# Gate and value of the first batch on 16-bit weight parts that later batches reuse, and the scores of two row blocks in one run

## The chip, the cores and the metric

One core of a Trainium2 chip runs the whole program. The metric is the time of one execution on the device in microseconds (us), as the median of the runs shown; one execution was recorded by the hardware profiler.

## What is computed

Four batches (B = 4) go through three blocks: causal attention over 8 heads of 64 with a second read from a memory matrix, a block of two linear maps whose product goes through w3 and w_out, and a gated block (gate, val, out).

```python
def _attn_ref(q, k, v, M_prev, z_prev, beta) -> np.ndarray:
    scores = scale * np.matmul(q, k.transpose(0, 1, 3, 2))
    ...
    a /= a.sum(-1, keepdims=True) + 1e-09
    local = np.matmul(a, v)
    ...
    return (g * mem_out + (1 - g) * local).astype(np.float32)

def _moe_ref(x, w1, w2, w3, w_out) -> np.ndarray:
    a = x @ w1
    b = x @ w2
    h = a * b @ w3
    return (h @ w_out).astype(np.float32)

def _moe2_ref(x, w_gate, w_val, w_out) -> np.ndarray:
    gate = 1.0 / (1.0 + np.exp(-(x @ w_gate)))
    val = x @ w_val
    return (gate * val @ w_out).astype(np.float32)
```

Each batch has 576 tokens of 512 features; w1 and w2 are 512 by 1024, gate and val 512 by 1536. The weights arrive as 64-bit numbers that the kernel itself converts to float32.

## The kernel before

**Products.** Every large product is split into parts: a weight is a large part plus a rest (`hi`, `lo`), an activation too, and `prod` issues three matmuls of 128x128 weights by 288 tokens (hi by hi, lo by hi, hi by lo). Parts are either float32 numbers rounded for the matmul unit (fp32r, `split_rows`: ScalarE casts, VectorE subtracts) or 16-bit floats after a multiplication by a power of two (`split_scaled`: ScalarE scales to the hi part, VectorE makes the rest). `power` works a scale out of a sum over partitions: `total` lets TensorE multiply a matrix of ones by one column, and four small VectorE instructions, each of which reads what the one before wrote, make the scale and its inverse.

**Stages.** `ffn(b)` runs four stages for batch b, and the trace shows each as one stretch of TensorE's time: `ab` (x by w1 and w2), `xw` (h by the product of w3 and w_out), `gv` (gate and val) and `ot` (the output map). In batch 0 the stretches are `ab` 118 to 219 us, `xw` 219 to 257, `gv` 257 to 334 and `ot` 334 to 386. The attention of batch b + 1 is fed into the stages of batch b piece by piece (`drive`), so its matmuls stand between those of the products; in the `gv` stages none does.

**Weights of batch 0.** A *unit* is 8 blocks of 128x128, for instance the gate and val blocks of one of the 12 column groups f. After every sixth matmul `pump` makes one step of each of three queues: `conv_step` converts half a unit from 64 bits (two ScalarE instructions, one VectorE instruction, and for `gv` units a VectorE maximum into `mcol`), `split_step` splits half a unit into fp32r parts in a ring of 5 slots (`wslot`), and `late_step` works on later batches' weights. In batch 0 one `gv` unit is two slots and one pass of f is 48 matmuls. Converted units are also stored whole (`kept`).

**Late tasks.** After batch 0's `gv` stage `late_scales` works out the scales of all 20 units of `ab` and `gv` at once. Then `late_split` reads the stored units back, 12 of them for `gv` first, makes 16-bit parts ("P", later sums "S") and stores these; batch 1 and later read them (`load_step`).

**PSUM.** Products and `total` take their banks from one pool, `ps_f`, of three buffers; which of them a tile gets is fixed when the program is built. A bank is free when ScalarE or VectorE has read what is in it. TensorE's order is the order written in the code. The other engines' orders are fixed when the program is built, and an engine that waits at one instruction starts none behind it.

**Scores.** `s_part(p, i, n)` makes the scores of row block i (116 rows, i + 1 column blocks) of the head pair p: three terms of two matmuls, one for each head, into two banks, then one VectorE instruction for each head, which adds the mask and takes the extreme value.

Of the kernel before, what the change touches and what calls it, by code (L numbers as in the profile page):

```python
# [19 lines left out]
T = 116  # L20
# [12 lines left out]
PB = 5  # L33
# [30 lines left out]
def tile_attention_memory_ffn(  # L64
# [178 lines left out]
    tasks = [(u, "P") for u in jobs[:F2]] + [(("o", *x), "P") for x in pairs_of]  # L243
# [135 lines left out]
    def conv_step():  # L379
# [27 lines left out]
        elif ws["step"] == 1:  # L407
# [50 lines left out]
    def split_step():  # L458
# [5 lines left out]
        u, hf = divmod(s, 2)  # L464
        r = raws[u][:, 4 * hf : 4 * hf + 4, :]
# [291 lines left out]
    def ffn(b):  # L757
# [3 lines left out]
        if b == 1:  # L761
            o2_scale()
            ws["limit"], ws["pace"] = NFIRST, PACE[5]
        if b == 2:
            ws["pace"] = PACE[3]
        if b > 0:
            htop = fp.tile([128, F1], F32, tag="htop", name=f"htop{b}", bufs=1)
        for f in range(F1):
# [36 lines left out]
            if b > 0:  # L805
                largest(htop[:, f : f + 1], hraw, AX.X)
# [12 lines left out]
        for d in range(KC):  # L819
            if b > 0 and d == 1:  # L820
                x2back = finish_x2(b, x2s)
                if b == 1:
# [698 lines left out]
```

## Time and profile before

| | us |
|---|---|
| three runs | 1014.47, 1018.92, 1017.41 (median 1017.41) |
| the profiled execution | 1013.13 |
| span from its first to its last instruction | 1011.3 |
| TensorE busy within the span | 982.4 (97%) |
| VectorE busy | 731.3 (72%) |
| ScalarE busy | 596.6 (59%) |
| GpSimd busy | 195.0 (19%) |

Busy time counts what an engine executes; a matmul is pipelined and the profile draws its end from a model, so that consecutive matmuls overlap and their spacing is read from start to start. Instructions of VectorE and ScalarE overlap too where they stand back to back.

### The profile page before, as it was taken

Reading aid. Unit: us, or ns where it says so; the run is one execution under the profiler, and the core shown is the slowest. Engines: PE = TensorE matmul, PEld = TensorE weight load, DVE = VectorE, ACT = ScalarE, POOL = GpSimd, SP = SyncE. Lnnn points to the kernel's source line nnn. Section 1 sums busy time; section 2 is a strip of 40 time slices with the busy share of each in tenths; the row PEclk is TensorE's granted clock in tenths of the full one; section 3 lists DMA queues with packets and bytes.
Section 4 is the critical chain, followed back from the end, with each engine's and each line's share of the span. In section 5 each row is a group of like instructions: output and inputs, shape, how many; then the busy total and the mean of one; then the engine's idle time right before and its main releaser. Section 6 shows DMA issues by size and latency. Waiting matters only on the chain. (4 is left out here: it accounts for less than half of the span.)

```text
span 1011.3 us, 19894 instructions
## 1 busy us (share of the span) xinstructions
PE 982.4 (97%) x7351; PEld 797.9 (79%) x7351; DVE 731.3 (72%) x1702; ACT 596.6 (59%) x1213; POOL 195.0 (19%) x196
## 2 busy tenths in 40 slices
PE   7999999999999999999999999999999999999998
PEld 3556687888999898898977777778777667797776
DVE  6866788777778826777777668988876757737883
ACT  7987787567777735564654545555655545324451
POOL 3454012213000101312200011343111311201110
PEclk9989999999999999999999999999999999999999
DMA  8865799967777249877887576655655556556532
GB/s 293 245 230 192 247 346 310 326 206 254 249 250 247 98 137 380 286 226 238 297 310 261 176 251 240 214 190 184 200 181 178 185 157 204 186 174 246 183 131 79
DMA packets 95642, 227.21 MB, mean 225 GB/s; under 512 B 11192, under 2 KB 39992, under 8 KB 95288
## 3 DMA queue, kind: packets, MB, share of 16 engines
q1 hardware_dynamic: 95544, 225.93, 66.3%
q8 instruction: 58, 0.95, 0.4%
q14 instruction: 40, 0.33, 0.1%
HBM read 164.55 MB, written 61.34 MB: 223 GB/s over the span
## 5 line engine op out<-in xcount | busy, mean ns | idle before, releaser
L532 PEld LDWEIGHTS <-wslot 128*128 128x128 f16 x1680 | 162.9, 98 | 49.7 <-issue 8.3
L1200 POOL TENSOR_SCALAR p<-p,sm,omg 116x116 f32<-116x116 f32 (+4 forms) x100 | 89.0, 895 | 406.2 <-DVE sm L1198 294.9
L521 PE MATMUL gv<-x,wslot 128*128 128x288 f32 (+1 forms) x1152 | 147.5, 290 | 0.2 <-ACT gsb L137 0.2
L521 PEld LDWEIGHTS <-wslot 128*128 128x128 f16 x1152 | 111.1, 98 | 32.1 <-issue 4.5
L532 PE MATMUL gvp<-x,wslot 128*128 128x288 f16 x1008 | 125.2, 286 | 3.6 <-ACT x L180 1.6
L137 ACT ACTIVATE p<-p,sm 116x116 f32<-116x116 f32 (+4 forms) x160 | 93.2, 585 | 46.6 <-DVE sm L1174 46.5
L521 PE MATMUL ot<-hg,wslot 128*128 128x288 f16 (+1 forms) x864 | 118.1, 291 | 0.0
L521 PE MATMUL ab<-x,wslot 128*128 128x288 f32 x768 | 117.2, 302 | 0.5 <-ACT asb L800 0.3
L521 PE MATMUL xw<-h,wslot 128*128 128x288 f32 x768 | 113.0, 300 | 1.7 <-ACT h L721 1.0
L521 PEld LDWEIGHTS ab<-x,wslot 128*128 128x128 f32 x768 | 104.0, 188 | 6.3 <-issue 2.9
L521 PEld LDWEIGHTS xw<-h,wslot 128*128 128x128 f32 x768 | 103.4, 188 | 5.5 <-issue 2.0
L1174 DVE CUSTOM_DVE_ANT_0 p<-s,msk 116x116 f32<-116x116 f32 (+4 forms) x160 | 68.0, 452 | 30.8 <-PE s L1169 26.8
L532 PE MATMUL abp<-x,wslot 128*128 128x288 f16 x672 | 87.1, 286 | 1.3 <-DVE u2ab L603 1.1
L723 DVE TENSOR_TENSOR wslot<-wraw,wslot 128x512 fp32r<-128x512 f32 x76 | 54.9, 725 | 34.7 <-ACT wslot L721 34.4
L521 PEld LDWEIGHTS gv<-x,wslot 128*128 128x128 f32 x576 | 76.4, 188 | 0.5 <-ACT gsb L137 0.5
L1230 PE MATMUL t<-idf,p 116*116 116x116 f32 x480 | 68.7, 272 | 3.3 <-DVE p L1200 2.5
L1230 PEld LDWEIGHTS t<-idf,p 116*116 116x116 f32 x480 | 54.3, 139 | 18.0 <-issue 5.3
L402 ACT ACTIVATE cy<-r 128x512 f32<-128x512 f32 x76 | 51.5, 678 | 13.3 <-DVE wraw L411 2.6
L721 ACT CAST wslot<-wraw 128x512 fp32r<-128x512 f32 x76 | 47.1, 621 | 16.2 <-PE gv L521 7.4
L411 DVE SCALAR_TENSOR_TENSOR wraw<-cy,cr 128x512 int32<-128x512 int32 x76 | 54.2, 740 | 2.6 <-ACT cr L403 2.1
L521 PE MATMUL wps<-wo,wslot 128*128 128x512 f32 x192 | 52.2, 407 | 0.0
L1248 ACT COPY pt<-t 116x696 f32<-116x696 f32 (+2 forms) x74 | 47.5, 650 | 7.4 <-PE t L1230 7.1
(210 smaller groups left out, 1630.0 us busy)
## 6 DMA issues: line engine op xcount, KB each, us to landing
wslot<-k SPq DMA_DIRECT2D x40, 512.0 KB, 4.3
wslot<-ka SPq DMA_DIRECT2D x40, 512.0 KB, 4.4
wrawl<-kf SPq DMA_DIRECT2D x32, 512.0 KB, 6.1
wslot<-kb SPq DMA_DIRECT2D x40, 384.0 KB, 3.5
k<-wslot SPq DMA_DIRECT2D x24, 512.0 KB, 4.7
r<-in_gv_dram SPq DMA_DIRECT2D x24, 512.0 KB, 5.1
kf<-wraw SPq DMA_DIRECT2D x20, 512.0 KB, 3.5
ka<-wS SPq DMA_DIRECT2D x20, 512.0 KB, 4.4
```

The source lines that it names most:

```text
L137: ins = nc.scalar.activation(**kw)
L402: nc.scalar.activation(out=y, in_=hi, func=AF.Prelu, scale=2.0**-112, alpha=2.0**32)
L411: nc.vector.scalar_tensor_tensor(z, y, 3, tmp["r"], ALU.logical_shift_left, ALU.bitwise_or)
L521: paced["pe"] = nc.tensor.matmul(ps, w[:, wi, blk, :], x[:, xi, cols : cols + n], start=first and part == 0, stop=last and part == 2,)
L532: paced["pe"] = nc.tensor.matmul(ps, w[:, wi, blk + k, :], x[:, xi, k, :], start=not more and k == 0 and part == 0, stop=k == 1 and part == 2,
L721: nc.scalar.copy(dst[:, 0], src)
L723: eng.tensor_sub(dst[:, 1], src, dst[:, 0].bitcast(F32))
L1174: nc.vector.tensor_tensor_reduce(out=ps_[hh][:, c0:c1], in0=os_[hh], in1=msk[:, SP - w + c0 : SP - w + c1], scale=-0.125, scalar=3.0e38 if ...
L1200: lower(SHARE_N).tensor_scalar(ps_[hh][:, :w], ps_[hh][:, :w], sm[:, 6 + hh : 7 + hh], omg[:T, 2 * p + hh : 2 * p + hh + 1], ALU.mult, ALU ...
L1230: nc.tensor.transpose(tp[:T, c : c + T], src[hh][:, j * T : (j + 1) * T], idf[:T, :T])
L1248: nc.scalar.copy(to, got)
```

## The change

In batch 0 the `gv` units are no longer split into fp32r halves. `scaled_step` works out a scale for each unit on its own (`unit_scale`: one `total` of two matmuls and the four small instructions), splits the whole unit in one go into 16-bit parts, which fill one slot of the ring, and stores them for the later batches. The 12 late tasks that made these parts are gone. Since 16-bit weights need 16-bit activations, the result of `xw` in batch 0 is scaled too, with a bound that needs the maximum of each h (`htop`) and the power of that bound. The scale of each unit enters the sigmoid and the product through `x2back`.

Apart from that, for batches 1 to 3 the scores of row blocks 0 and 1 are made in one run of twelve matmuls into the same two banks. The pool of score tiles grows from 5 to 6, and q's natural-order tile goes from two buffers to one.

```diff
-    tasks = [(u, "P") for u in jobs[:F2]] + [(("o", *x), "P") for x in pairs_of]
+    tasks = [(("o", *x), "P") for x in pairs_of]
...
+    def unit_scale(u):
+        n = rank[u]
+        power(wsc[:, n : n + 1], wsc[:, NJ + n : NJ + n + 1], total(f"wsum{n}", *(mcol[:, hf, n : n + 1] for hf in range(2))))
+        scaled.add(u)
+
+    def scaled_step(u, now):
+
+        if ws["conv"] < 2 * u + 2:
+            return False
+        if u not in scaled:
+            if not now and ws["pumps"] < ws["ready"]:
+                return False
+            unit_scale(u)
+            return True
+        if in_use("wslot") >= RING:
+            return False
+        w = fp.tile([128, 2, 8, 128], F16, tag="wslot", name=f"wslot{ws['ring']}", bufs=RING)
+        split_scaled(w[:, 0], w[:, 1], raws.pop(u), wsc[:, rank[u] : rank[u] + 1])
+        nc.sync.dma_start(out=whole16[u]["P"], in_=w)
+        done.append((u, "P"))
+        put("wslot", [w])
+        ws["split"] += 2
+        return True
...
+        if u in rank and rank[u] < F2:
+            return scaled_step(u, now)
...
-            if b > 0:
-                largest(htop[:, f : f + 1], hraw, AX.X)
+            largest(htop[:, f : f + 1], hraw, AX.X)
...
-                if b == 0:
-                    nc.scalar.copy(xt[:, 0, c0 : c0 + HS], ps[:, :HS])
-                    nc.vector.tensor_sub(
-                        xt[:, 1, c0 : c0 + HS], ps[:, :HS], xt[:, 0, c0 : c0 + HS].bitcast(F32)
-                    )
-                elif b == 1 and d == 0:
+                if b < 2 and d == 0:
                     nc.scalar.copy(x20[:, c0 : c0 + HS], ps[:, :HS])
-                elif b == 1:
+                elif b < 2:
                     split_scaled(xt[:, 0, c0 : c0 + HS], xt[:, 1, c0 : c0 + HS], ps[:, :HS], x2s[:, 0:1])
...
+            s = take(1)
+            if b == 0:
+                slot(s)
+                nc.vector.tensor_mul(x2back[:, f : f + 1], wsc[:, NJ + f : NJ + f + 1], x2s[:, 1:2])
...
+            if i == 1 and not first:
+                return
+            rows = (0, 1) if i == 0 and not first else (i,)
```

**VectorE in the `gv` stage.** Before, one pass of f looks like this on VectorE (`wslot` is the rest of half a unit, `hgraw` the gated product, `wraw` a conversion, `mcol` a maximum, `hg` the rest of the gated activations):

```order
L964 TENSOR_TENSOR hgraw0_5_3659<-gv0_5_0_1_3687,gsb0_5_0_3685 128x288
L723 TENSOR_TENSOR wslot55_3726<-wraw31_3495,wslot55_3726 128x512
L964 TENSOR_TENSOR hgraw0_5_3659<-gv0_5_1_1_3719,gsb0_5_1_3717 128x288
L411 SCALAR_TENSOR_TENSOR wraw34_3753<-cy68_3735,cr68_3736 128x512
L411 SCALAR_TENSOR_TENSOR wraw34_3753<-cy69_3765,cr69_3766 128x512
L723 TENSOR_TENSOR wslot56_3756<-wraw32_3581,wslot56_3756 128x512
L176 TENSOR_REDUCE mcol_86<-wraw34_3753 128x1
L723 TENSOR_TENSOR hg0_5_3658<-hgraw0_5_3659,hg0_5_3658 128x576
L176 TENSOR_REDUCE mcol_86<-wraw34_3753 128x1
```

With the change, early in the same stage, `pw`, `wsc` and `x2back0` being the small instructions of a scale (the first `wsc` row of each `pw` makes the scale, the second its inverse):

```order
L164 TENSOR_SCALAR wsc_83<-pw_3354 128x1
L165 TENSOR_SCALAR pw_3354<-wsc_83 128x1
L985 SCALAR_TENSOR_TENSOR hgraw0_0_3286<-gv0_0_1_1_3344,x2back0_2897,gsb0_0_1_3342 128x288
L166 TENSOR_SCALAR wsc_83<-pw_3354 128x1
L163 TENSOR_SCALAR pw_3391<-wsum4_3388 128x1
L969 TENSOR_TENSOR x2back0_2897<-wsc_83,x2s0_2813 128x1
L164 TENSOR_SCALAR wsc_83<-pw_3391 128x1
L181 SCALAR_TENSOR_TENSOR wslot43_3365<-wraw27_3111,wsc_83,wslot43_3365 128x1024
L165 TENSOR_SCALAR pw_3391<-wsc_83 128x1
L749 TENSOR_TENSOR hg0_0_3285<-hgraw0_0_3286,hg0_0_3285 128x576
L439 SCALAR_TENSOR_TENSOR wraw30_3402<-cy60_3382,cr60_3383 128x512
L166 TENSOR_SCALAR wsc_83<-pw_3391 128x1
```

The two halves became one instruction of twice the width, and the small instructions of two scales stand around it. The rest `wslot43` reads ScalarE's hi part of the same unit, and that hi part reads the scale of the first row shown; `wslot44`, whose scale is the `wsc` row just ahead of `wslot43`, follows two rows after the last one shown.

**ScalarE at the start of `gv`.** Before, `wslot` being the hi part of half a unit, `x2_0_3` the last block of `xw`, `cy` and `cr` a conversion and `gsb` a sigmoid, with the load of its table ahead of the first:

```order
L841 CAST x2_0_3_3155<-xw0_3_0_3156 128x288
L721 CAST wslot43_3205<-wraw25_2856 128x512
L721 CAST wslot44_3229<-wraw26_2992 128x512
L841 CAST x2_0_3_3155<-xw0_3_1_3192 128x288
L402 ACTIVATE cy58_3305<-r64_58_3167 128x512
L403 ACTIVATE cr58_3306<-r64_58_3167 128x512
L402 ACTIVATE cy59_3335<-r64_59_3218 128x512
L403 ACTIVATE cr59_3336<-r64_59_3218 128x512
L137 ACT_TABLE_LOAD
L137 ACTIVATE gsb0_0_0_3258<-gv0_0_0_0_3236 128x288
```

With the change:

```order
L180 ACTIVATE wslot41_3210<-wraw25_2864,wsc_83 128x1024
L180 ACTIVATE x2_0_3_3182<-xw0_3_0_3183,x2s0_2813 128x288
L180 ACTIVATE wslot42_3246<-wraw26_3028,wsc_83 128x1024
L430 ACTIVATE cy58_3277<-r64_58_3140 128x512
L431 ACTIVATE cr58_3278<-r64_58_3140 128x512
L180 ACTIVATE x2_0_3_3182<-xw0_3_1_3236,x2s0_2813 128x288
L430 ACTIVATE cy59_3304<-r64_59_3224 128x512
L431 ACTIVATE cr59_3305<-r64_59_3224 128x512
L137 ACT_TABLE_LOAD
L137 ACTIVATE gsb0_0_0_3310<-gv0_0_0_0_3288,x2back0_2897 128x288
```

Two hi parts of whole units, each behind the scale that VectorE makes, stand ahead of the table load, and one of them ahead of the last block's first half. In the program as built, `gv0_0_1_0` (the gate product of the second token half) has the bank of `gv0_0_0_0` with the change, and so waits for the first sigmoid; before it had a bank of its own, and the product behind it waited for that sigmoid.

**TensorE, scores of batch 2, pair 1.** Before, row block 0 is one run and row block 1 another, with products between them:

```order
L1169 MATMUL s2_1_0_0_0_5250<-qkh2_1_5194,qkl2_1_5195 116x116
L1169 MATMUL s2_1_0_0_1_5251<-qkh2_1_5194,qkl2_1_5195 116x116
L1169 MATMUL s2_1_0_0_0_5250<-qkl2_1_5195,qkh2_1_5194 116x116
L1169 MATMUL s2_1_0_0_1_5251<-qkl2_1_5195,qkh2_1_5194 116x116
...
L1169 MATMUL s2_1_1_0_0_5321<-qkh2_1_5194 116x232
L1169 MATMUL s2_1_1_0_1_5322<-qkh2_1_5194 116x232
L1169 MATMUL s2_1_1_0_0_5321<-qkh2_1_5194,qkl2_1_5195 116x232
L1169 MATMUL s2_1_1_0_1_5322<-qkh2_1_5194,qkl2_1_5195 116x232
```

With the change they stand in one:

```order
L1201 MATMUL s2_1_1_0_0_5348<-qkl2_1_5289,qkh2_1_5288 116x116
L1201 MATMUL s2_1_1_0_1_5349<-qkl2_1_5289,qkh2_1_5288 116x116
L1201 MATMUL s2_1_1_0_0_5348<-qkh2_1_5288 116x232
L1201 MATMUL s2_1_1_0_1_5349<-qkh2_1_5288 116x232
L1201 MATMUL s2_1_1_0_0_5348<-qkh2_1_5288,qkl2_1_5289 116x232
L1201 MATMUL s2_1_1_0_1_5349<-qkh2_1_5288,qkl2_1_5289 116x232
L1201 MATMUL s2_1_1_0_0_5348<-qkl2_1_5289,qkh2_1_5288 116x232
```

The first run's last pair is followed at once by the second block's first.

## Rows read from the trace of the kernel before

**Rows 1.** Windows: busy time, granted clock and DMA load in five stretches
```profile
core 0: us, PE busy (x) PEld busy (x) DVE busy (x) ACT busy (x) POOL busy (x), PEclk, DMA share, GB/s
219.00:257.00 38.00, 36.34 (x282) 32.29 (x281) 30.39 (x74) 26.79 (x58) 9.86 (x8) 1.00 0.75 260
257.00:334.00 77.00, 76.76 (x580) 76.53 (x578) 60.52 (x109) 58.15 (x110) 0.00 (x0) 1.00 0.72 245
334.00:386.00 52.00, 50.84 (x378) 46.84 (x378) 24.52 (x51) 25.24 (x45) 6.00 (x4) 0.97 0.41 139
386.00:466.00 80.00, 79.29 (x618) 69.42 (x618) 59.38 (x160) 48.17 (x106) 22.12 (x20) 1.00 0.81 282
...
347.60:351.00 3.40, 3.40 (x17) 3.07 (x18) 3.40 (x9) 1.25 (x2) 1.19 (x1) 0.51 0.40 154
```

**Rows 2.** Groups by line and shape: the `gv` matmuls on fp32r and 16-bit parts
```profile
L521 PE MATMUL gv<-x,wslot 128*128 128x288 f32 x576 | 76.7, 295 | 0.2 <-ACT gsb L137 0.2
L521 PE MATMUL gv<-x,wslot 128*128 128x288 f16 x576 | 70.8, 286 | 0.0
```

**Rows 3.** Timeline of VectorE over one pass of f in batch 0
```profile
283.42 0.45 DVE L964 TENSOR_TENSOR hgraw<-gv,gsb 128x288 f32<-128x288 f32 x1
283.79 1.28 DVE L411 SCALAR_TENSOR_TENSOR wraw<-cy,cr 128x512 int32<-128x512 int32 x2
284.99 0.68 DVE L723 TENSOR_TENSOR wslot<-wraw,wslot 128x512 fp32r<-128x512 f32 x1
285.59 0.68 DVE L176 TENSOR_REDUCE mcol<-wraw 128x1 bf16<-128x512 f32 x1
286.19 0.75 DVE L723 TENSOR_TENSOR hg<-hgraw,hg 128x576 fp32r<-128x576 f32 x1
...
287.45 0.45 DVE L964 TENSOR_TENSOR hgraw<-gv,gsb 128x288 f32<-128x288 f32 x1
289.17 0.69 DVE L723 TENSOR_TENSOR wslot<-wraw,wslot 128x512 fp32r<-128x512 f32 x1 [1.27 <-ACT wslot L721]
```

**Rows 4.** Timeline of VectorE and ScalarE where batch 1 makes its x2 scale
```profile
475.54 0.14 DVE L163 TENSOR_SCALAR pw<-x2sum 128x1 int32<-128x1 int32 x1
475.72 0.15 DVE L164 TENSOR_SCALAR x2s<-pw 128x1 f32<-128x1 f32 x1
...
475.99 0.78 ACT L180 ACTIVATE x<-x,x2s 128x576 f16<-128x576 f32 x1
```

**Rows 5.** Timeline of VectorE in batch 1's `gv` stage
```profile
521.11 0.51 DVE L960 SCALAR_TENSOR_TENSOR hgraw<-gv,x2back,gsb 128x288 f32<-128x288 f32 x1
521.53 0.14 DVE L1030 TENSOR_SCALAR hgs<-hgs 128x1 f32<-128x1 f32 x1
521.61 1.28 DVE L181 SCALAR_TENSOR_TENSOR wS<-wrawl,wsc,wS 128x1024 f16<-128x1024 f32 x1
522.81 0.81 DVE L181 SCALAR_TENSOR_TENSOR hg<-hgraw,hgs,hg 128x576 f16<-128x576 f32 x1
```

**Rows 6.** Groups by line and shape: ScalarE's part of a 16-bit split
```profile
L180 ACT ACTIVATE wP<-wrawl,wsc 128x1024 f16<-128x1024 f32 x12 | 13.8, 1148 | 4.9 <-DMA wrawl<-kf 4.9
```

**Rows 7.** Timeline of TensorE and ScalarE at the start of batch 0's `gv` stage
```profile
257.27 4.92 PE L521 MATMUL gv<-x,wslot 128*128 128x288 f32 x36
262.42 3.84 PE L521 MATMUL gv<-x,wslot 128*128 128x288 f32 x27 [0.24 <-ACT gsb L137]
...
260.67 1.28 ACT L137 ACT_TABLE_LOAD   x1
261.96 0.71 ACT L137 ACTIVATE gsb<-gv 128x288 f32<-128x288 f32 x2
```

**Rows 8.** Timeline of TensorE around a score block in batch 1's `ab` stage
```profile
418.84 2.24 PE L521 MATMUL ab<-x,wslot 128*128 128x288 f32 x15
421.00 0.37 PE L1169 MATMUL s<-qkh 64*116 64x232 f32 x2
```

**Rows 9.** Timeline of TensorE at a wait in batch 0's `ot` stage
```profile
347.06 0.90 PE L1169 MATMUL s<-qkh 64*116 64x290 f32 x2 [1.16 <-DVE sm L1174]
```

More of the change, by code (lines that the diff above doesn't have):

```diff
@@ L271, in tile_attention_memory_ffn @@
     wot = {}
-    ws = {"conv": 0, "step": 0, "split": 0, "ring": 0, "freed": 0, "use": 0, "again": 0, "pumps": 0, "late": 0, "task": 0, "part": 0, "limit": 0, "pace": 0, "tops": 0, "wo": 0, "pass": 0, "wready": False}
+    ws = {"conv": 0, "step": 0, "split": 0, "ring": 0, "freed": 0, "use": 0, "again": 0, "pumps": 0, "late": 0, "task": 0, "part": 0, "limit": 0, "pace": 0, "ready": 0, "tops": 0, "wo": 0, "pass": 0, "wready": False}
     tmp = {}
+    scaled = set()
     last = {}
@@ L327, in late_split @@
         late_o2 = u not in rank
+        if late_o2 and "o2" not in scaled:
+            scaled.add("o2")
+            o2_scale()
+            return
         by = o2s[:, 0:1] if late_o2 else wsc[:, rank[u] : rank[u] + 1]
@@ L456, in load_step, with split_step @@
         return True
-    def split_step():
+    def split_step(now=False):
         s = ws["split"]
@@ L1173, in s_part @@
[L1173 to L1183 removed]
+            if i == 1 and not first:
+                return
@@ new lines, in s_part @@
+            os_ = [
+                ps_s.tile([128, 512], F32, tag="s", name=f"s{b}_{p}_{i}_{n}_{hh}")[:T, :at] for hh in range(2)
+            ]
+            terms = [(qks[p], qks[p])] if first else [(parts[p][x], parts[p][y]) for x, y in ((0, 0), (1, 0), (0, 1))]
+            for i, w, c0, c1, at in jobs:
+                for x, (q_, k_) in enumerate(terms):
+                    for hh in range(2):
+                        r = slice(64 * hh, 64 * hh + 64)
+                        nc.tensor.matmul(
+                            os_[hh][:, at : at + c1 - c0], q_[r, 0, i * T : (i + 1) * T], k_[r, 1, c0:c1],
+                            start=x == 0, stop=x == len(terms) - 1,
+                        )
@@ new lines, in s_part @@
+            for i, w, c0, c1, at in jobs:
+                ps_, sm = sp[p, i]
+                for hh in range(2):
+                    nc.vector.tensor_tensor_reduce(
+                        out=ps_[hh][:, c0:c1],
+                        in0=os_[hh][:, at : at + c1 - c0],
+                        in1=msk[:, SP - w + c0 : SP - w + c1],
+                        scale=-0.125,
+                        scalar=3.0e38 if n == 0 else sm[:, 2 * hh : 2 * hh + 1],
+                        op0=ALU.add,
+                        op1=ALU.min,
+                        accum_out=sm[:, 2 * hh + n : 2 * hh + n + 1],
+                    )
```

110 lines of the change are left out of this document (45 added, 65 removed).

## The prediction, made before the changed kernel ran

> **What bounds the kernel now.** The table of the profile comes first: TensorE is busy in 97% of the span, so a change counts where it alters what TensorE executes or makes it wait. Next come the windows, one for each stage [rows 1]. In batch 0's `gv` stage (257 to 334 us) TensorE is busy for 76.76 of 77.00 us at full granted clock, VectorE for 60.52, ScalarE for 58.15, and DMA at a share of 0.72. So TensorE sets the pace there, one pass of f in 6.4 us, and VectorE, with 79%, is the engine with the least room. The groups by line [rows 2] hold what the change can gain: the same 576 matmuls take 76.7 us on fp32r parts in batch 0 and 70.8 us on 16-bit parts in batch 1, 133 against 123 ns each. With 16-bit parts TensorE wants a pass in 5.9 us.
>
> The timeline of VectorE [rows 3] shows what one pass costs there, read from start to start, since durations overlap by about 0.08 us: two conversions 1.20, two rests of half a unit 1.20, two maxima 1.20, two `hgraw` 0.74, one `hg` 0.67: 5.0 us of work in 6.4. The rest is waiting, for example 1.27 us for ScalarE's hi part of a `wslot`.
>
> **The change, part by part.** The sum is made against the profiled execution, 1013.13 us, which is 4.3 us below the median of the runs, 1017.41; the differences are then laid on the median.
>
> *Matmuls of `gv`.* -5.9 us on TensorE [rows 2], if it is fed. Nine of the twelve pairs that sum for the scales stand in this stage. No row has such a pair; two matmuls at 133 ns give 0.27 as an upper bound, and nothing is the lower one; I take 0.1 each, since they have one column instead of 288. So TensorE would need 71.7 us.
>
> *VectorE in `gv`.* From the first half of `hgraw0_0` to the rest `wslot51`, the last split, VectorE's list in the changed program holds 16 conversions and 18 maxima at 0.60 [rows 3], 16 `hgraw` that now multiply by `x2back` as well, at 0.42 (521.11 to 521.53 [rows 5]), 7 `hg` at 0.67, 9 rests of whole units at 1.20 (521.61 to 522.81 [rows 5]), and 46 small instructions. The first five kinds come to 9.6 + 10.8 + 6.7 + 4.7 + 10.8 = 42.6 us. The grouping itself gains nothing here: two halves cost 1.20 and so does a whole. A small instruction takes 0.08 us with independent work behind it (521.53 to 521.61 [rows 5]) and 0.18 where the next reads its result (475.54 to 475.72 [rows 4]): 3.7 to 8.3 us for 46. Some stand in a chain and others between large instructions, so I take 6.0.
>
> A rest also waits for ScalarE's hi part, and that for the scale: 0.27 us from the scale's instruction to ScalarE's start (475.72 to 475.99 [rows 4]) and 1.15 for the hi part [rows 6], 1.42 in all, less what VectorE does meanwhile. Behind the scale of `wslot43` stand one `hgraw` and five small instructions, about 1.07, so a wait of 0.35; `wslot45` is alike, and before `wslot51` there is about 0.8, a wait of 0.6. Before the other six stands a whole split, an `hg` or a conversion, more than 1.42. That is 1.3 us, if ScalarE comes to the hi part at once. Sum: 42.6 + 6.0 + 1.3 = 49.9 us.
>
> TensorE consumes eight units meanwhile, for which it would need 47.8. So **VectorE becomes the pace of these eight units**, barely. How much it idles besides is not to be read: nothing at best, and at worst the 1.3 to 1.4 us that each pass idles now, 10 us for eight. Most of that idling exists because TensorE is the pace now, so it should shrink; I take 3.8.
>
> *The start of `gv`.* ScalarE loads its table (1.28 us) ahead of the first sigmoid, which starts 4.69 us after the stage's first matmul; TensorE goes on 5.15 us after it [rows 7]. Today that costs 0.24 us, because 36 matmuls run before its result frees a bank. In the changed program the third product has the bank of the first, so 24 matmuls run, 2.95 us. At an unchanged time of the sigmoid that is a wait of 2.2 us. The two hi parts of whole units in front take 1.15 each instead of 0.62 for halves, so it could come 1.1 us later (3.3); or earlier, as the scales of these units are summed long before the stage begins and ScalarE can do both hi parts in `xw` (1.1). I take 2.2: VectorE's row above then starts 5.15 us into the stage.
>
> *The stage's end.* 5.15 + 49.9 + 3.8 = 58.9 us for the rest `wslot51`. The last read of unit 7's products stands 2.2 us ahead of it (three small instructions, the wait, the split), at 56.7. TensorE is by then perhaps one product (1.5 us) into unit 8 and has four units to do, 23.6 us, for which VectorE has no splits left: 56.7 - 1.5 + 23.6 = 78.8. That is **2.0 us longer than today's 76.8**: the gain of 5.9 is spent. Without idling it is 75.0, with all of it 85.2.
>
> *A rule on small instructions.* The Trainium skill, page "Perfetto Trace Analysis", section "Optimizing Scalar/DVE Operations", gives about 60 ns of overhead for each VectorE instruction on SBUF and says that grouping helps a saturated engine. By it the 46 would cost 2.8 us instead of 6.0, and the stage would come out at 75.6, which makes the whole 1014.5. The row of independent work (0.08) is near it and the row of a dependent chain (0.18) is not; these are chains.
>
> *`xw` of batch 0.* VectorE has one maximum more ahead of what `xw` begins with (0.60 [rows 3]), and the bound and its power follow; then three sums for scales stand in the stage. VectorE is at 80% in `xw` [rows 1]. I take +0.8 us, between 0 and 2.
>
> *`ab` of batch 0.* Eight maxima for `htop`, 4.8 us of VectorE, hidden by its idle time; in batch 1's `ab` VectorE is busy for 59.38 of 80 us [rows 1]. +0.3, at most 4.8 if that cover is gone.
>
> *The late tasks.* Twelve hi parts (13.8 us [rows 6]) and twelve rests (14.4) vanish. They lie in `ot` of batch 0 and `ab` of batch 1, where ScalarE and VectorE have room and TensorE is idle for 1.16 and 0.71 us only [rows 1]: 0, at best -1.9. The 12 loads go too, and the stores move into `gv`.
>
> *Scores in one run.* TensorE needs 2.16 us for 15 matmuls up to a score block [rows 8], 0.165 us more than 15 times 133 ns: the price of turning to another shape. A run spared saves that once, or twice if turning back costs as much: 12 head pairs (three batches) make 2.0 to 4.0 us; I take -2.8. VectorE's first mask instruction then comes six matmuls later; the next products of that bank pair are further away. q's single buffer could delay a load; nothing shows that, and I put it at 0.
>
> **Sum:** +2.0 + 0.8 + 0.3 - 2.8 = +0.3 us, 1013.4 for the profiled execution, **1018 us** on the median.
>
> **The rivals.** *VectorE keeps up (faster).* If it hardly idles and the first sigmoid comes early, `gv` takes 71.7 plus about 1.1: -4.0. With +1.1 for `ab` and `xw`, -2.8 for the scores and -1.9 for the late tasks this is -7.6, 1010 us. For it: eight units need 47.8 against 49.9 us, close. Against it: VectorE is at no more than 80% in any whole stage of [rows 1]. It decides if VectorE's work and waits of one unit stay below 5.9 us. Chance 0.16.
>
> *The way through ScalarE becomes the bound (slower).* The 1.42 us are hidden only if ScalarE takes up each hi part as soon as its scale is there. ScalarE's list has sigmoids, conversions and `hg` ahead of it. If it comes to each hi part late, VectorE stands still for 1.42 at each of the nine splits: 12.8 instead of 1.3. Replacing the 3.8 of idling too, `gv` takes 86.5, +9.7, and the whole +8.0, 1025 us. For it: VectorE waits 1.27 us for ScalarE's hi part already now, with half the width [rows 3]. Against it: ScalarE is busy for only 58.15 of 77 us [rows 1]. It decides if three or more of the splits show such a wait over 1 us. Chance 0.22. The Trainium skill ("Perfetto Trace Analysis", section "Per-instruction lifecycle: what the profiler-reported window actually captures") calls the queues of these two engines strict FIFO; that is this rival's rule, and the trace agrees so far as that 1.27 us wait holds up everything behind it.
>
> *The DMA becomes the bound (slower).* 245 GB/s at a share of 0.72 [rows 1] make about 340 at a full one. A unit now moves 1.05 MB in, 0.52 out as before, and 0.52 of 16-bit parts out: 2.1 MB, 6.2 us. Conversions run up to a unit further ahead than before; nine units of it take 55.8 us less 4.7 for what the three load buffers hold, 51, against VectorE's 49.9. At worst it adds 5 us: 1023. Chance 0.10.
>
> *Waits bring the clock down (slower).* After the 1.16 us wait at 347.06 [rows 9] the granted clock is 0.51 for 3.4 us [rows 1], the lower level of 1.2 GHz, which costs 1.7 us. Five waits of that length in `gv` would add 8.5: 1026. In today's `gv` the clock stays at 1.00. Chance 0.08.
>
> That the change doesn't do what it says is hardly possible: batch 1 runs the same matmuls at 16 bits already.
>
> **How the numbers follow.** The forecast (VectorE paces at about the old rate) has 0.44. 0.5%, or 5.1 us, is about what a measurement of this kernel can tell from no change. Faster by more: 0.16, the first rival. Slower by more: the ScalarE and the clock rival, half of the DMA rival, less a bit for their mild forms, 0.31. Within: 0.53. The likeliest case's own range is 1013 to 1023 (idling from 0 to 8 us in `gv`); for 8 in 10 it reaches to the first rival below and beyond the ScalarE rival above: **1010 to 1029**.
>
> **What would show it.** In the changed profile: 576 16-bit matmuls in batch 0's `gv`, with about 123 ns each where they run unhindered; a wait on a sigmoid of some 2 us in front of the third product; VectorE busy above 85% until `wslot51`, TensorE waiting for `hgraw` or sigmoids in these units and not in the last four; the stage some 79 us long; 12 fewer score runs. I am wrong if `gv` is below 74 or above 84 us, or if a stage that I left alone moves by more than 2 us: then a cover that I named, or the single buffer of q, was not as I read it.

## The result: slower by about 4 us, and the profile after

The changed kernel takes 1020.71 us (median of 8 runs, 1016.85 to 1027.84), the kernel before 1016.74 (8 runs). The medians differ by 4.0 us, or 0.4%; the ratio taken over all runs is 1.0058, with a 95% interval from 1.003 to 1.0086. The profiled execution is a long one, 1025.5 us with a span of 1023.4, 12.2 us above the one before, so much of what its rows show is more than the median lost.

The lengths of the stages, from the first matmul of one to the first of the next in the two profiled executions, say where to look:

| us | before | after |
|---|---|---|
| last map ahead of `ab`, batch 0 | 6.5 | 5.8 |
| `ab`, batch 0 | 101.2 | 111.5 |
| `xw`, batch 0 | 38.2 | 41.3 |
| `gv`, batch 0 | 76.9 | 77.6 |
| `ot`, batch 0 | 51.6 | 49.5 |
| `ab`, batch 1 | 80.8 | 79.0 |
| `ab`, batch 2 | 59.4 | 62.2 |

The stage that the change is about hardly moved. Two others grew: `ab` of batch 0 and `xw` of batch 0. The windows of the changed kernel (us; busy time of each engine; granted clock; DMA share; GB/s) answer to [rows 1]; the first three are `ab`, then come `xw`, `gv` and `ot`, and apart from these most of the first eight units of `gv` and the last four:

```profile
core 0: us, PE busy (x) PEld busy (x) DVE busy (x) ACT busy (x) POOL busy (x), PEclk, DMA share, GB/s
119.00:140.00 21.00, 17.34 (x104) 14.41 (x102) 15.80 (x34) 14.82 (x32) 1.77 (x2) 0.92 0.98 356
140.00:165.00 25.00, 20.81 (x125) 17.74 (x127) 21.47 (x47) 18.31 (x39) 6.45 (x5) 0.89 0.90 297
165.00:230.60 65.60, 63.86 (x472) 54.71 (x468) 47.21 (x112) 36.85 (x82) 9.36 (x8) 0.99 0.72 245
230.60:272.00 41.40, 38.37 (x289) 33.96 (x289) 34.87 (x98) 29.03 (x58) 9.48 (x8) 0.96 0.76 271
272.00:349.50 77.50, 71.93 (x596) 56.79 (x595) 67.47 (x148) 61.01 (x103) 0.00 (x0) 1.00 0.86 315
349.50:399.00 49.50, 48.88 (x375) 45.03 (x374) 23.00 (x50) 22.79 (x40) 5.98 (x4) 1.00 0.40 135
...
276.78:328.00 51.22, 46.58 (x391) 36.66 (x390) 45.70 (x111) 39.80 (x65) 0.00 (x0) 1.00 0.94 349
328.00:349.50 21.50, 21.50 (x178) 17.19 (x176) 16.99 (x28) 16.45 (x31) 0.00 (x0) 1.00 0.64 237
```

In the first two, TensorE is idle for 7.9 of 46 us and its clock is down to 0.92 and 0.89; in `xw` it is at 0.96. Over the whole of `ab` TensorE's idle time grew by 6.6 us (from 3.1 to 9.7), and its busy time, for the same matmuls, by 3.7: in three stretches, from 128.9, 142.6 and 163.0 us on, the granted clock is 0.50 or 0.51, the lower of the two levels (1.2 GHz). `xw` has one such stretch, from 238.1. Before, neither stage has any. In `gv` TensorE is busy for 71.93 us, as 16-bit matmuls should be, and idle for 5.6.

**`gv` went nearly as written.** Groups by line of TensorE in `gv` of the changed kernel, which answer to [rows 2]:

```profile
L552 PE MATMUL gv<-x,wslot 128*128 128x288 f16 x576 | 72.0, 286 | 4.8 <-ACT gsb L137 4.8
L172 PE MATMUL wsum<-mcol,ones 128*128 128x1 bf16 x18 | 1.7, 165 | 0.8 <-ACT gsb L137 0.8
```

Its waits in the timeline (start, duration, in brackets the idle time ahead and what ended it):

```profile
276.08 2.37 PE L552 MATMUL gv<-x,wslot 128*128 128x288 f16 x18 [0.93 <-ACT gsb L137]
292.94 6.87 PE L552 MATMUL gv<-x,wslot 128*128 128x288 f16 x54 [1.80 <-ACT gsb L137]
301.18 0.90 PE L552 MATMUL gv<-x,wslot 128*128 128x288 f16 x6 [0.59 <-ACT gsb L137]
311.73 1.63 PE L552 MATMUL gv<-x,wslot 128*128 128x288 f16 x12 [1.46 <-ACT gsb L137]
322.31 0.19 PE L172 MATMUL wsum<-mcol,ones 128*128 128x1 bf16 x2 [0.80 <-ACT gsb L137]
```

All five are put down to a sigmoid and lie in the first eight units. VectorE's timeline at its first `hgraw` and at the three splits that waited for ScalarE, the last being `wslot51`:

```profile
276.09 0.51 DVE L985 SCALAR_TENSOR_TENSOR hgraw<-gv,x2back,gsb 128x288 f32<-128x288 f32 x1
...
293.95 1.28 DVE L181 SCALAR_TENSOR_TENSOR wslot<-wraw,wsc,wslot 128x1024 f16<-128x1024 f32 x1 [0.27 <-ACT wslot L180]
...
305.75 1.28 DVE L181 SCALAR_TENSOR_TENSOR wslot<-wraw,wsc,wslot 128x1024 f16<-128x1024 f32 x1 [0.97 <-ACT wslot L180]
...
327.76 1.28 DVE L181 SCALAR_TENSOR_TENSOR wslot<-wraw,wsc,wslot 128x1024 f16<-128x1024 f32 x1 [0.35 <-ACT wslot L180]
```

By the last two windows VectorE is busy for 89% of the first eight units (45.70 of 51.22 us). Its list from `hgraw0_0` to the rest of `wslot51` takes from 276.09 to about 328.97, 52.9 us. In the last four units TensorE never waits.

**`xw`: two longer waits.** Timeline of TensorE and VectorE at the last h of batch 0, in the changed kernel:

```profile
235.76 0.74 DVE L176 TENSOR_REDUCE htop<-hraw 128x1 f32<-128x576 f32 x1
...
237.17 0.75 DVE L749 TENSOR_TENSOR h<-hraw,h 128x576 fp32r<-128x576 f32 x1
...
236.08 0.53 PE L552 MATMUL xw<-h,wslot 128*128 128x288 f32 x2 [1.52 <-ACT h L747]
...
237.98 0.49 PE L552 MATMUL xw<-h,wslot 128*128 128x288 f32 x1 [1.38 <-DVE h L749]
```

The new maximum stands ahead of the rest that TensorE waits for. Before, the same two waits were 0.96 and 0.70 us:

```profile
223.74 0.53 PE L521 MATMUL xw<-h,wslot 128*128 128x288 f32 x2 [0.96 <-ACT h L721]
...
224.97 0.40 PE L521 MATMUL xw<-h,wslot 128*128 128x288 f32 x1 [0.70 <-DVE h L723]
```

**`ab`: waits for the softmax of batch 1.** Timeline of all engines at the longest wait of the stage:

```profile
158.85 1.91 POOL L1136 TENSOR_TENSOR me<-mphi,z 116x640 f32<-116x640 f32 x1 [11.11 <-DVE mphi L1134]
...
159.37 1.43 DVE L1231 TENSOR_SCALAR sm<-sm 116x2 f32<-116x2 f32 x1
160.71 1.28 DVE L439 SCALAR_TENSOR_TENSOR wraw<-cy,cr 128x512 int32<-128x512 int32 x2
...
161.91 0.38 DVE L1234 TENSOR_SCALAR p<-p,sm,omg 116x116 f32<-116x116 f32 x1
...
162.44 0.38 PE L1264 MATMUL t<-idf,p 116*116 116x116 f32 x2 [3.29 <-DVE p L1234]
```

VectorE scales p of the first row block only at 161.91, behind two conversions of weights; TensorE stood still for 3.29 us. In the whole stage it waits 7.5 us for p on VectorE (2.3 before) and 2.0 for the scores' banks (0.4 before). The first theories were therefore about the merged scores (M) and about the eight maxima (H).

### The profile page after: what moved, and what is told of

Read it like the earlier page. It is cut to its first block, busy times and chain, and to the rows that moved or that the text cites. A ratio compares the mean times of both kernels' runs of the same rounds, so it can differ in the third digit from the quotient of the medians.

```text
span 1023.4 us, 19906 instructions
## 1 busy us (share of the span) xinstructions
PE 980.4 (96%) x7375; PEld 781.6 (76%) x7375; DVE 739.9 (72%) x1752; ACT 587.3 (57%) x1190; POOL 196.3 (19%) x196
## 5 line engine op out<-in xcount | busy, mean ns | idle before, releaser
L552 PEld LDWEIGHTS <-wslot 128*128 128x128 f16 x1728 | 166.8, 98 | 51.4 <-issue 9.9
L563 PEld LDWEIGHTS <-wslot 128*128 128x128 f16 x1680 | 163.2, 98 | 52.3 <-issue 11.6
L552 PE MATMUL gv<-x,wslot 128*128 128x288 f16 x1152 | 142.8, 286 | 4.8 <-ACT gsb L137 4.8
L430 ACT ACTIVATE cy<-r 128x512 f32<-128x512 f32 x76 | 51.6, 678 | 23.9 <-DVE wraw L439 7.4
L749 DVE TENSOR_TENSOR wslot<-wraw,wslot 128x512 fp32r<-128x512 f32 x52 | 38.9, 749 | 22.9 <-ACT wslot L747 20.7
L431 ACT ACTIVATE cr<-r 128x512 int32<-128x512 uint32 x76 | 50.9, 670 | 0.0
L1332 PE MATMUL o<-pt,vs 116*64 116x344 f32 (+2 forms) x320 | 50.7, 423 | 0.0
```

The lines of the kernel that those rows point to most:

```text
L430: nc.scalar.activation(out=y, in_=hi, func=AF.Prelu, scale=2.0**-112, alpha=2.0**32)
L431: nc.scalar.activation(out=r, in_=w[:, :, 0].bitcast(U32), func=AF.Copy, scale=LAST3, bias=HALF)
L552: paced["pe"] = nc.tensor.matmul(ps, w[:, wi, blk, :], x[:, xi, cols : cols + n], start=first and part == 0, stop=last and part == 2,)
L563: paced["pe"] = nc.tensor.matmul(ps, w[:, wi, blk + k, :], x[:, xi, k, :], start=not more and k == 0 and part == 0, stop=k == 1 and part == 2,
L749: eng.tensor_sub(dst[:, 1], src, dst[:, 0].bitcast(F32))
L1332: nc.tensor.matmul(ot[r, XO + q0 : XO + S], v_[:, j, hh], pt[:, hh, j].rearrange("p a c -> p (a c)")[:, q0 - X : S - X] if j < 4 else pt[: ...
```

## The experiments

All ratios are to the kernel before, run on the same chip. "ab 0" and the like are stage lengths of the one profiled execution, and a single execution can be some us off its kernel's median.

| kernel | ratio | 95% interval | ab 0 | xw 0 | gv 0 | ab 2 |
|---|---|---|---|---|---|---|
| changed kernel | 1.0058 | 1.003 to 1.0086 | 111.5 | 41.3 | 77.6 | 62.2 |
| e1: scores, six score tiles, one q | 1.0019 | 0.9994 to 1.0044 | 103.0 | 38.1 | 76.9 | 62.7 |
| e2: gv, six tiles, one q | 1.0087 | 1.0063 to 1.0111 | 103.6 | 41.7 | 76.2 | 62.6 |
| e3: gv, five tiles, two q | 1.0003 | 0.9983 to 1.0022 | 100.9 | 42.5 | 76.6 | 59.4 |
| e4: changed, scores in batches 2, 3 | 1.0081 | 1.0058 to 1.0104 | 105.4 | 42.9 | 77.0 | 62.2 |
| e5: gv, five tiles, one q | 1.0086 | 1.0061 to 1.011 | 104.1 | 41.7 | 77.9 | 60.4 |
| e6: gv, scores, five tiles, two q | 1.0105 | 1.0079 to 1.0132 | 109.8 | 42.0 | 76.8 | 61.7 |
| e7: e3, last maximum moved | 0.9981 | 0.9963 to 0.9998 | 101.3 | 39.1 | 76.0 | 59.4 |
| e8: e6, last maximum moved | 1.009 | 1.0059 to 1.0121 | 107.5 | 38.5 | 76.2 | 61.7 |
| e9: e5, q loaded by GpSimd | 1.0069 | 1.0042 to 1.0095 | 106.9 | 42.5 | 77.0 | 59.7 |
| e10: changed, q by GpSimd, maximum moved | 1.0139 | 1.0111 to 1.0166 | 108.9 | 40.1 | 77.2 | 62.7 |
| e11: e7, one scale for all units | 0.9998 | 0.9981 to 1.0014 | 100.7 | 43.9 | 73.0 | 59.4 |
| e12: e7, scores in batches 2, 3 | 0.9997 | 0.998 to 1.0014 | 101.8 | 39.1 | 76.2 | 61.7 |

### The parts one by one (e1 to e4)

e1 is the kernel before with the new `s_part`, and with

```diff
-PB = 5
+PB = 6
-                q_ = ap.tile([128, NT, 2, D], F32, tag="qnr", name=f"qnr{b}_{p}")
+                q_ = ap.tile([128, NT, 2, D], F32, tag="qnr", name=f"qnr{b}_{p}", bufs=1)
```

> The kernel before with nothing but the scores of row blocks 0 and 1 in one run, six score tiles and one buffer for q's natural-order tile. Theory M (the merged run is what makes batch 0's ab stage longer, since that stage carries batch 1's attention and VectorE is close to full there; in the later batches it saves what was forecast): ab of batch 0 takes 105 to 112 us instead of 101, the rest of the program 2 to 4 us less, and the whole is 1 to 7 us above the kernel before (1.001 to 1.007). Rival H (the eight maxima for htop and the other instructions of the gv change make ab longer): ab of batch 0 stays at 101 to 102 us and the whole is 2 to 4 us below the kernel before.

e2 is the changed kernel with the scores in two runs:

```diff
-            if i == 1 and not first:
-                return
-            rows = (0, 1) if i == 0 and not first else (i,)
+            rows = (i,)
```

> The changed kernel with the scores of row blocks 0 and 1 in two runs as before; the six score tiles and q's single buffer stay. Theory M: ab of batch 0 is back at 101 to 103 us, gv of batch 0 stays at 77 to 79, and the whole is within 2 us of the kernel before. Rival H: ab of batch 0 stays at 107 us or more and the whole is 5 to 9 us above the kernel before, since the gain of the merged scores in later batches is gone too.

e3 is e2 with `PB = 5` and two buffers for q's tile.

> The changed kernel with the scores in two runs, five score tiles and two buffers for q's tile: the gv part of the change alone. If the buffers matter (a third theory, B: q's single buffer delays batch 1's attention in ab of batch 0), ab of batch 0 is 101 to 102 us here and longer by 3 us or more in the run that keeps the single buffer. Under theory M both runs agree within 1 us; under rival H both have an ab of 107 us or more.

e4 has the merged scores in batches 2 and 3 only (`b > 1` in place of `not first`).

> The changed kernel with the merged scores in batches 2 and 3 only; batch 1, whose attention is fed into batch 0's stages, has two runs as before. Theory M: ab of batch 0 at 101 to 103 us, the later stages as in the changed kernel, and the whole 3 to 6 us below the changed kernel, at 0.997 to 1.001 of the kernel before. Rival H: the whole within 1 us of the changed kernel.

e1's time, 1.0019, lies in M's range, but its `ab` of 103.0 us is shorter than M's 105 to 112 and longer than H's 101 to 102. M fell with the other two: without merged scores (e2) the time was not lower, and e4 gained nothing. H fell with e3, which has all eight maxima and the whole gv change and stands at 1.0003 with an `ab` of 100.9 us. What set e2 and e3 apart is the sixth score tile and q's buffer, 0.0084 of the time, 8.5 us. The third theory, B, was right in that a buffer decides. The gv part alone neither gains nor loses.

### Which buffer, and why (e5, e9, e10)

e5 is e3 with one buffer for q's tile (the `bufs=1` above).

> The gv part alone with five score tiles and a single buffer for q's tile. Theory B1 (the single buffer costs the time: the load of the next pair's q can be issued only when VectorE has read the last one, and on SP's queue it holds up the weight loads and stores behind it): 6 to 9 us above the kernel before (1.006 to 1.009), and ab of batch 2 at about 62 us instead of 59.4. Rival P (the sixth score tile moved the work): within 2 us of the kernel before, as the run with two buffers, and ab of batch 2 at 59.4.

It measured 1.0086: **in the gv part alone q's single buffer costs all of the 8.5 us, the sixth score tile nothing that can be told** (e2 has both and stands at 1.0087; in their traces VectorE and ScalarE of e2 and e5 execute the same list in the same order). The windows of e3 and e5, the last map ahead of `ab`, `ab` of batch 0 and `ab` of batch 2 of each:

```profile
111.91:118.38 6.47, 6.47 (x34) 4.97 (x32) 5.34 (x12) 5.89 (x14) 0.00 (x0) 1.00 0.81 255
118.38:219.30 100.92, 97.88 (x698) 83.41 (x697) 85.02 (x196) 69.53 (x151) 18.12 (x16) 1.00 0.88 308
624.30:683.80 59.50, 58.25 (x482) 43.30 (x480) 52.98 (x147) 34.22 (x85) 24.28 (x23) 1.00 0.68 224
```

```profile
115.17:123.78 8.61, 6.73 (x34) 4.92 (x32) 6.14 (x13) 5.80 (x14) 0.00 (x0) 1.00 0.92 291
123.78:227.84 104.06, 98.69 (x698) 83.30 (x696) 83.83 (x194) 70.74 (x154) 17.57 (x16) 1.00 0.83 291
633.10:693.50 60.40, 58.25 (x481) 43.20 (x479) 52.88 (x147) 34.16 (x85) 24.27 (x23) 1.00 0.67 219
```

The spans of these two executions differ by 10.1 us, and no single long wait holds them: 2.1 us ahead of `ab`, 3.1 in `ab` of batch 0, 1.3 in `gv`, 0.9 in `ab` of batch 2, where the forecast of 62 was wrong, and `xw` is 0.8 shorter. Another 3.1 us lie further ahead, in the stretch up to the last map (82.9 and 86.0 us), where e5's granted clock is 0.92 and e3's 0.96; kernels with two buffers take 82.9 to 86.5 us there, so this part can't be put down to the buffer. The wait ahead of `ab` can be read: TensorE waits in e5 for the rest of a weight part, `wo`, that VectorE makes.

```profile
120.46 0.50 PE L552 MATMUL wps<-wo,wslot 128*128 128x512 f32 x1 [1.88 <-DVE wo L749]
```

VectorE's order at this rest, in e5 and then in e3 (the second row of each pair comes behind the first on the engine):

```profile
119.41 0.39 DVE L1206 CUSTOM_DVE_ANT_0 p<-s,msk 116x232 f32<-116x232 f32 x1
...
119.72 0.69 DVE L749 TENSOR_TENSOR wo<-wraw,wo 128x512 fp32r<-128x512 f32 x1
```

```profile
114.04 0.68 DVE L749 TENSOR_TENSOR wo<-wraw,wo 128x512 fp32r<-128x512 f32 x1
114.68 0.40 DVE L1206 CUSTOM_DVE_ANT_0 p<-s,msk 116x232 f32<-116x232 f32 x1
```

In e3 the rest stands ahead of the two masks of a score block, in e5 behind both and behind a maximum. ScalarE's part of `wo` was done at 117.24 in e5, so this wait of 1.88 us, of the 2.1 that the stretch lost, comes from VectorE's order and not from a late load. e2, with the same order, has it too (1.9 us).

e9 took the load off SP's queue:

```diff
-                nc.sync.dma_start(out=q_, in_=qn[b, p])
+                nc.gpsimd.dma_start(out=q_, in_=qn[b, p])
```

> The gv part alone with one buffer for q's tile, whose load is now issued by GpSimd and no longer on SP's queue. Theory B1 (the load waits on SP's queue and holds up the weight loads and stores behind it): back to the run with two buffers, 1.000 to 1.003 of the kernel before, with 6.5 us instead of 8.6 in the stretch ahead of ab of batch 0 and 59.4 in ab of batch 2. Rival B2 (q itself comes too late for the memory read, whichever queue it stands on): still 1.006 or more.

e10 did the same in the changed kernel, with the maximum moved as in e7 below.

> The changed kernel, merged scores and six score tiles included, with the load of q's tile issued by GpSimd and the maximum of the last h of batch 0 behind its rest. Under B1 and W: 8 to 10 us below the changed kernel, 0.996 to 0.999 of the kernel before. Under B2: 2 us below the changed kernel, 1.003 to 1.005.

B1's forecasts fell: e9 stays at 1.0069, and e10 came out at 1.0139, which neither theory allows for; e10 is the slowest of all. The traces agree: from 28 us to the end of `ab` of batch 0, SP stands for VectorE ahead of q's load for 9.4 us in e3 and 10.9 in e5, hardly longer. B2 forecast e9's time, but its reason isn't in the traces: in `ab` of batch 0 VectorE waits for no load of q, in e5 and in e9; its waits for q, 4.9 us in all of e5 and 2.0 in e9, lie elsewhere, and in e3 there is one, of 0.9. Only in `ab` of batch 2 of e5 does one of 1.0 us stand beside a stage that is 0.9 longer.

There is a third reading: one buffer changes the order in which the program is built. Between the traces of e3 and e5 some 175 of VectorE's 1752 instructions stand elsewhere in its list, and some 86 of ScalarE's 1190. The wait for `wo` above is of this kind. Between e5 and e9 as many of VectorE's stand elsewhere, so e9 changed more than the queue. That the other order is what costs the rest of the 8.5 us as well is likely, but not shown: no run has one buffer and the order of two.

### Merged scores (e6, e8, e12)

e6 is the changed kernel with `PB = 5` and two buffers for q's tile.

> The changed kernel with two buffers for q's tile and five score tiles: gv part and merged scores. Theory B1 with a gain of the merged scores: 1 to 3 us below the run of the gv part alone, 0.997 to 1.000 of the kernel before, ab of batch 0 at 101 to 103 us. Rival M2 (the merged scores cost by themselves, since the softmax of the first block comes later than its transposes want it): 2 to 5 us above the kernel before, with waits of over 2 us for p in ab of batch 0.

e8 is e6 with the maximum moved.

> The gv part, the merged scores, two buffers for q's tile, five score tiles, and the maximum of the last h behind its rest. Under B1 and W the effects add up: 2 to 6 us below the kernel before (0.994 to 0.998). Under M2 or V it stays within 2 us of the kernel before or above it.

e12 is e7 with merged scores in batches 2 and 3 only.

> The gv part with the maximum of the last h behind its rest, two buffers for q's tile, five score tiles, and merged scores in batches 2 and 3 only. If the merged scores cost only in ab of batch 0, where the weights are converted (theory M3): within 2 us of the same kernel without merged scores, 0.996 to 1.000 of the kernel before, ab of batch 0 at 101 us. If five score tiles are too few for merged scores everywhere (rival M4): 3 us or more above it, with ab of batches 1 and 2 longer.

With five tiles and two q buffers the merged scores cost 0.0102, 10 us (e6 against e3), and e8, at 1.009, is like it. M2 had the direction, but not the size (2 to 5 us) and not the reason: the longest wait for p in this `ab` is 1.6 us, hardly longer than e3's 1.5, and the longest of all is not for p. The sum that e8 was to show did not come. In the changed kernel (six tiles, one q) they may even gain: 1.0058 against e2's 1.0087, with intervals that overlap. e12 shows where: in batches 2 and 3 they cost nothing that can be told (0.9997 against e7's 0.9981, overlapping). They don't gain there either: `ab` of batch 2 grew from 59.4 to 61.7 us, which is more than the 0.6, 0.3 and 0.7 that `ab` and `xw` of batch 1 and `xw` of batch 2 gave back. So most of e6's loss comes with batch 1's attention, which runs inside batch 0's stages. The row of `ab` in e6, and waits there, VectorE's for a weight and TensorE's for ScalarE:

```profile
122.73:232.51 109.78, 101.74 (x698) 86.94 (x697) 84.11 (x194) 69.76 (x150) 16.93 (x16) 0.95 0.82 285
```

```profile
123.12 0.69 DVE L774 TENSOR_TENSOR wpart<-wps,wpart 128x512 f32<-128x512 f32 x1 [2.52 <-DMA r<-in_w_dram]
...
130.73 1.09 PE L552 MATMUL ab<-x,wslot 128*128 128x288 f32 x3 [3.41 <-ACT asb L824]
```

Ahead of TensorE's wait VectorE stands 2.52 us and ScalarE 1.41 us behind loads, and in the stage the clock is down to 0.95 on average. Why merged scores lead into these waits is open. That they hold four score tiles at once, and that five are too few, was not tried by itself: no run has six tiles and two q buffers.

### The last maximum (e7)

```diff
             split_rows(ht, hraw, SHARE_H)
-            largest(htop[:, f : f + 1], hraw, AX.X)
+            top = largest(htop[:, f : f + 1], hraw, AX.X)
+            if b == 0 and f == F1 - 1:
+                tc.add_manual_dep(top.ins, last["rest"].ins.name, ...)
```

> The gv part alone, with the maximum of the last h of batch 0 put behind that h's rest on VectorE. Theory W (in xw of batch 0 the two waits for the last h, 1.4 and 1.4 us, are what bring the clock down, and the maximum makes the second one longer by 0.6): the second wait is 0.7 us as in the kernel before, xw takes 39 to 41 us instead of 42.5, and the whole is 1 to 3 us below the run of the gv part alone. Rival V (the first wait, for ScalarE's cast, suffices for the clock to fall): xw loses the 0.6 us of the wait alone and stays above 41 us.

Theory W's numbers came true. e3's two waits at the last h, e7's timeline there, and the windows of `xw` in e3 and in e7:

```profile
224.42 0.53 PE L552 MATMUL xw<-h,wslot 128*128 128x288 f32 x2 [1.41 <-ACT h L747]
226.32 0.61 PE L552 MATMUL xw<-h,wslot 128*128 128x288 f32 x1 [1.37 <-DVE h L749]
```

```profile
227.32 0.65 ACT L747 CAST h<-hraw 128x576 fp32r<-128x576 f32 x1
...
228.03 0.53 PE L552 MATMUL xw<-h,wslot 128*128 128x288 f32 x2 [1.15 <-ACT h L747]
...
228.46 0.75 DVE L749 TENSOR_TENSOR h<-hraw,h 128x576 fp32r<-128x576 f32 x1
229.13 0.74 DVE L176 TENSOR_REDUCE htop<-hraw 128x1 f32<-128x576 f32 x1
229.26 0.40 PE L552 MATMUL xw<-h,wslot 128*128 128x288 f32 x1 [0.70 <-DVE h L749]
```

```profile
219.30:261.78 42.48, 39.70 (x291) 35.04 (x289) 34.19 (x95) 29.34 (x59) 9.37 (x8) 0.92 0.73 264
```

```profile
223.17:262.25 39.08, 37.23 (x291) 32.72 (x290) 33.14 (x95) 29.29 (x59) 9.06 (x8) 1.00 0.81 287
```

One instruction of 0.74 us (0.67 from start to start) behind another instead of ahead of it gave 3.4 us in the stage: 0.9 from the two waits (1.41 and 1.37 in e3) and the rest from the clock, 0.92 on average in e3 and 1.00 in e7. e7 is the fastest kernel of this study, 2 us below the kernel before, with an interval that just excludes no change; against e3 the intervals overlap.

The traces of all kernels bear W out, but not as a rule without exception. Where the second wait is 1.30 to 1.38 us (the changed kernel, e2 to e6, e9) the clock fell behind it in seven of seven. Where it is 0.70 to 0.72 (before, e1, e7, e8, e12, and e10 and e11) it stayed up in five of seven, and fell in e10 and e11. e11's two waits and the window right behind them:

```profile
227.39 0.53 PE L555 MATMUL xw<-h,wslot 128*128 128x288 f32 x2 [0.95 <-ACT h L750]
228.62 0.40 PE L555 MATMUL xw<-h,wslot 128*128 128x288 f32 x1 [0.71 <-DVE h L752]
```

```profile
229.20:232.60 3.40, 3.40 (x19) 3.08 (x18) 2.06 (x9) 3.00 (x8) 1.31 (x1) 0.50 0.84 342
```

So the shorter wait makes the fall rarer and doesn't exclude it.

### What fills `gv` (e11)

```diff
-        power(wsc[:, n : n + 1], wsc[:, NJ + n : NJ + n + 1], total(f"wsum{n}", *(mcol[:, hf, n : n + 1] for hf in range(2))))
+        if n == 0:
+            power(wsc[:, :1], wsc[:, NJ : NJ + 1], total(f"wsum{n}", *(mcol[:, hf, n : n + 1] for hf in range(2))))
+            for c in (0, NJ):
+                nc.vector.tensor_copy(wsc[:, c + 1 : c + F2], wsc[:, c : c + 1].to_broadcast([128, F2 - 1]))
```

> The gv part alone with the maximum of the last h behind its rest, and the scale of the first gv unit used for all twelve: eleven sums on TensorE and 44 small VectorE instructions are left out, so the scales of the other units aren't their own. Theory S (the scale chains are what keeps gv of batch 0 at 76 us where the matmuls need 71): 72.5 to 74 us in gv and TensorE's waits there below 2 us in all. Rival Q (ScalarE's order and the banks set the waits): gv within 1 us of 76.

`gv` of e11 in the windows, and the only wait of TensorE in it:

```profile
266.60:339.56 72.96, 70.76 (x579) 56.39 (x578) 61.88 (x96) 58.53 (x100) 0.00 (x0) 1.00 0.88 322
```

```profile
271.92 67.78 PE L555 MATMUL gv<-x,wslot 128*128 128x288 f16 x552 [2.20 <-ACT gsb L137]
```

Theory S was right: 73.0 us, and after the first sigmoid TensorE runs 552 matmuls without a wait (the one ahead of them, 2.20, is a little above the 2 that S allowed). Nine pairs of sums on TensorE are gone from the stage as well, but they take about 0.05 us each (a pair at 278.28 in the changed kernel, the next matmul at 278.33), 0.5 us of the 3.1. So making a scale for each unit is what eats most of the gain of the 16-bit parts; e11 doesn't tell the 44 small instructions themselves from what waits for their result. The whole didn't follow (0.9998). In `xw` of the profiled execution the clock fell twice, at the last h as shown above and behind a new wait of 2.12 us for batch 1's softmax, and the stage took 43.9 us; whether that is the whole reason one execution doesn't show.

## Why the prediction held in `gv` and not elsewhere, point by point

The time, 1020.7, lies in the range (1010 to 1029) and 2.7 us above the forecast of 1018. The forecast side ("within 0.5%") and "slower by more" cannot be told apart: the interval has the bound in it. The sum was nearer than its terms, and that is luck: in the two profiled executions `ab` of batch 0 is 10.3 us longer, where the sum has 0.3 and at most 4.8, and `xw` 3.1, where it has at most 2; the stages behind `gv` gave back about 3. By the prediction's own sign, a stage that it left alone and that moves by more than 2 us, it was wrong outside `gv`.

*Matmuls of `gv`, VectorE's pace: right.* 71.93 us of work on TensorE against 71.7; VectorE's list of eight units in 52.9 us against 49.9 + 3.8 = 53.7; the rest `wslot51` done 56.9 us into the stage against 58.9; busy at 89% until there, no wait of TensorE behind it; the stage 77.6 against 78.8. e11 shows the cause by taking the scales away. The waits of the three splits were 0.27, 0.97 and 0.35 for the forecast 1.3 in all, though one is on another slot; a fourth split waited 0.36 us, put down to a DMA. The Trainium skill's 60 ns ("Perfetto Trace Analysis", section "Optimizing Scalar/DVE Operations") would have put the stage at 75.6: the measured one lies 2.0 us above that and 1.2 below the sum from the rows.

*The start of `gv`: mis-sized.* 0.93 us in the changed kernel, where I took 2.2 from a range down to 1.1: ScalarE did the hi parts early. In e11 the same wait is 2.20.

*`xw`: the step that named the term but not its size.* +0.8, at most 2; measured +3.1, and +4.3 in e3. The maximum ahead of the last rest was seen; that two waits of 1.4 us bring the clock down was only weighed as a rival for `gv`. The clock rival came true in the wrong stages, here and in `ab` of batch 0, and not in `gv` (1.00).

*`ab` of batch 0: the eight maxima cost nothing* (e3), as the cover that I named allowed, though the row that I took for it is of batch 1; in batch 0 VectorE is busy for 80.2 of the stage's 101 us. The 10.3 us come from the rest of the change: longer waits for p and the scores' banks, and the clock. Which of its parts brings them is not settled: without merged scores in batch 1 (e4) the stage takes 105.4 us, without any (e2) 103.6, and neither kernel is faster as a whole.

*q's single buffer: the step that failed.* "nothing shows that, and I put it at 0": with the gv part alone it costs about 8.5 us (e5 against e3). It was a term without a row, and had neither an upper bound nor a chance. What it costs in the changed kernel no run shows: e1, with one buffer and without the gv part, stands at 1.0019, and e6, which has the second buffer back and the sixth tile gone, is slower than the changed kernel.

*The scores: -2.8 was right at best by luck.* In the changed kernel they may have brought about that much (e2 to the changed kernel, not resolved); in e6 the same code costs 10 us, and in batches 2 and 3 alone (e12) nothing was gained. The saving at the switch is small: `xw` of batch 2 fell from 39.8 to 39.1 us in e12, and `ab` of batch 2 rose by 2.3. Most of the loss is in `ab` of batch 0, around the softmax, where the forecast didn't look.

*The late tasks: 0, at best -1.9.* In e3, which has the gv part alone, `ot` of batch 0 and `ab` of batch 1 are 0.7 and 1.1 us shorter (50.9 and 79.7): near the better bound. The 0.7 are the clock's, though: `ot` has 0.97 before and 1.00 in e3, where TensorE is idle for longer (2.0 us against 1.2).

*The rivals.* VectorE kept up less than the first one needed. The way through ScalarE never waited 1 us at a split: fell. The DMA was at 0.94 in the eight units, close to its bound; nothing shows that it set the time.

## What to carry to other kernels

Price every edit that pays for another one's memory: here a buffer given up for a score tile cost 8.5 us in the gv part alone, where what the tile was for saved 3 at best. A buffer count also changes the order in which the engines' lists are built, so compare the lists, and not only the waits for that buffer. Where an engine's list is fixed, look for the instruction that TensorE waits for and put new work behind it; 0.7 us moved gave 3.4 in one stage. A faster matmul moves the bound to whatever prepares its operands, so count that engine's chains of small instructions before the matmuls.

## What the runs showed of the hardware

*Waits and the clock.* In `xw` of batch 0, waits of 0.96 and 0.70 us (before) and of 1.15 and 0.70 (e7) left the granted clock at 1.00 of full speed; 1.41 and 1.37 (e3) brought the stage's mean to 0.92, that is for a part of it to the lower of the two levels. Waits of 0.95 and 0.71 (e11) brought it down as well, so the two lengths alone don't decide. The runs' mean clocks say what this is worth in the whole: the changed kernel's has a median of 0.989, that of the kernel before 0.992 to 0.993 in the sets run beside e1 to e12. By an estimate from these two, 0.003 to 0.004 of 1020 us, or 3 to 4 us, are what the clock can have cost: as much as the medians differ. e5's is 0.992 and the kernel before's beside it 0.992, so its loss is one of waits in the main; e6's is 0.986, which by the same estimate is 6 of its 10 us.

*A small VectorE instruction that ended with GpSimd's.* In the timeline of `ab` above, `sm` on 116x2 elements lasts 1.43 us, where the one at 157.89 lasts 0.16. It ends at 160.80, and a GpSimd instruction of 1.91 us at 160.76. The Trainium skill ("Perfetto Trace Analysis", section "Optimizing Scalar/DVE Operations") says that the two engines share a read port; the row agrees, but no run here took GpSimd's instruction away.
